# Two probability-value products behind each other in an attention plus SwiGLU kernel

## The chip, the cores and the metric

The kernel runs on one core of a Trainium2 chip. A core has a matrix engine (PE, which loads weights with its own instruction, PEld), a vector engine (DVE), a scalar engine (ACT), a general engine (POOL) and a queue engine (SP) that here only issues DMAs. PE writes to PSUM, eight banks of 512 fp32 columns over 128 partitions; DVE and ACT move results from there to SBUF. Each engine runs its own instructions in the order of the program, and semaphores keep them in step. The metric is the device time of one execution in microseconds: 559.44 us, median of three runs (559.44 to 559.45).

## What is computed

The reference, cut to what matters (S = 2048 tokens, D = 576, H = 32 heads of 18, window W = 256, F = 4608):

```python
xn = layernorm(x)
q, k, v = split(xn @ wqkv)                  # 32 heads of 18
p = softmax(where(0 <= i - j < 256, q @ k.T * 18 ** -0.5, -1e9))
a = (p @ v) @ wo
h = silu(xn @ w1) * (xn @ w3)
out = x + a + h @ w2
```

## The kernel before, in words

The tokens are taken in four chunks of 512 (c = 0 to 3). A chunk has three stretches on PE. First come the projections of q, k and v (chunk 0's stand ahead of the loop). Then come 36 *units* (u = 0 to 35), one for each 128 of the 4608 hidden features. Then a second phase, here called p2, multiplies the hidden features hT by w2 and the attention's output oT by wo, both into the same four PSUM banks, and writes the chunk out.

**A unit** is nine pairs of matmuls, n = 0 to 8 (`unit_pairs`, L697). Each pair uses the two halves of the array at once, 64 rows each, with 512 columns of tokens; one half of the pair makes the gate, the other the up product, in two PSUM banks. Then ACT makes a tanh of the gate (`unit_tanh`, L706), and two DVE instructions make gs and then hT (`unit_h`, L712 and L715). The attention is dealt out between these pairs, so that ACT, DVE and POOL have time for it.

**Attention.** The 32 heads form eight groups g of four. For a group and a chunk there are five steps (four in chunk 0). A step is a few score matmuls into PSUM banks 6 and 7 (`scores`, L571), one exp on ACT (`exps`, L580, from both banks into one *slot* of 1024 bf16 per partition) and one or two masks on POOL (L607). When both groups of a pair j are through, a *PV* (`pv`, L628) multiplies the probabilities with the values. It uses another split of the array: eight tiles of 64 rows and 20 columns, 96 matmuls in chunks 1 to 3, 72 in chunk 0, into two banks. A chunk has four PVs, j = 0 to 3. The last one stands at the start of p2, behind four small matmuls (`wo_rest`, L683).

**Behind a PV** DVE transposes both banks out (`pv_out`, L637, into the buffers `uqs`, the second of which lies in the output tiles `ofin`); then for each half a reciprocal on DVE (L642) and a product on POOL (`o_scale`, L643) and transposes back in two halves per group (`o_turn`, L650, called turns here) into `od`. DMAs pack `od` into oT (`o_pack`, `o_rest`). `later(u, ...)` puts these off, so that they stand behind `unit_h` of unit u, u + 1, u + 2 and u + 3.

**PSUM banks.** Six banks form three pairs that `job()` hands out in turn: to units, PVs and projections. So a unit or a PV takes the banks of the third last one, and PE waits until DVE has read these.

**The order** is written by a planner. `clock` counts time on PE in pair times: 1 for a pair or a step of scores, 6.6 for a PV. `spaced_step` (L955) spreads the steps of scores evenly over what is left of the chunk, at least 7.5 apart, as long as a slot is free; one may also be put ahead of a unit's last pair. A PV is put behind the first unit that ends 20 after the last step that it needs:

```python
if next_pv in pv_ready and clock >= pv_ready[next_pv] and next_pv < 3:
    ...
    later(u, lambda b=banks: (pv_out(b[0], 0), pv_out(b[1], 1), o_scale(0)))
```

In chunks 1 and 2 the planner puts the PVs 0, 1 and 2 behind units 8, 16 and 24, in chunk 3 behind 8, 17 and 26.

**Slots.** The first four steps of a chunk use the hT tiles of units 28 to 35, which are written only then. After that come ten slots of `pt` and, in chunks 1 to 3, four in `stage`; a PV gives its `pt` and `stage` slots back.

**DMAs.** SP issues nearly all of them in order, each after the semaphores that it needs. w1 and w3 come in parts (`load_part`), w2 in 72 tiles of 512 x 288, 288 KB each, through four buffers: whenever p2 is through with a tile, `load_w2` (L338, called in `p2_item`) loads the one four further on, at the end of p2 the first four of the next chunk. Chunk 0's first four load at units 20 to 26.

**The next chunk's tokens** are normalised during the units: statistics at units 20, 24, 30 and 34 (`ln_stats`, L353 to L356), applied at 22, 26, 32 and 35 (`ln_apply`, L378) on DVE, and turned by a DMA (`xn_send`) at 23, 27, 33 and in p2. Chunk 3 has none of this.

## Time and profile before

| what | value |
|---|---|
| median of three runs | 559.44 us |
| span of the profiled execution | 557.72 us |
| PE busy | 553.1 us, 99% |
| DVE, ACT, POOL busy | 309.6, 259.4, 163.3 us |
| chain that ended last | PE 98%, DMA 1% |
| granted PE clock | 9 tenths or more in all 40 slices |
| DMA, mean | 154 GB/s |
| w2 tile, issue to landing | 3.4 us median |

The profile is of one execution. Its span, 557.72 us, is 1.72 us less than the runs' median; the rest lies ahead of its first and behind its last instruction. The page reports matmuls as busy from their start to a modelled end, so overlapping matmuls make PE look busy throughout. Lost time on PE is therefore read from the starts: a matmul of N columns keeps its part of the array for N columns, and what lies beyond that until the next start is lost. The line with the chain says what the end of the kernel hung on. In lines of the timeline the first number is the start in us, the second the length, and a bracket at the end says how long the engine was idle before it and what released it.

### The profile page before, as it was taken

The page shows a single profiled execution, that of the slowest core. Times are in us where ns is not written, and L with a number is a line of the kernel's source. Part 1 is how long each engine was busy: PE and PEld are TensorE (multiplying, and loading weights), DVE is VectorE, ACT ScalarE, POOL GpSimd, SP SyncE. Part 2 cuts the span into 40 slices and gives each one's busy share as a digit, 9 for nine tenths or more (in the row PEclk, how much of TensorE's full clock was granted, in tenths as well). Part 3 has the DMA queues.
Part 4 walks back from the last instruction along what each step waited for, and adds up shares of the span by engine and source line. Part 5 has one row for each costly group of instructions (what it writes and reads, how often), then busy time and mean ns, then how long its engine had stood idle before and what let it go on. Part 6 is the DMA issues. An engine that isn't in the chain of part 4 may idle for free.

```text
span 557.7 us, 15727 instructions
## 1 busy us (share of the span) xinstructions
PE 553.1 (99%) x6766; PEld 332.9 (60%) x6766; DVE 309.6 (56%) x578; ACT 259.4 (47%) x357; POOL 163.3 (29%) x389
## 2 busy tenths in 40 slices
PE   8999999999999999999999999999999999999998
PEld 4445545787655455477764554548776555455776
DVE  6465889610365778851056668884105577777211
ACT  6457776100387776500048777650005776765000
POOL 5513454300034445330003444423001343432000
PEclk9999999999999999999999999999999999999999
DMA  9987989978576358466956744966593673562552
GB/s 234 228 177 179 207 141 196 165 201 225 135 139 146 110 139 188 125 144 174 238 107 139 166 115 113 182 153 140 151 249 78 135 172 98 129 142 54 139 149 65
DMA packets 127072, 85.96 MB, mean 154 GB/s; under 512 B 34179, under 2 KB 124763, under 8 KB 127003
## 3 DMA queue, kind: packets, MB, share of 16 engines
q1 hardware_dynamic: 125011, 82.69, 64.5%
q10 hardware_dynamic: 1992, 2.27, 1.7%
q8 instruction: 53, 0.87, 0.7%
q14 instruction: 16, 0.13, 0.1%
HBM read 71.29 MB, written 2.36 MB: 132 GB/s over the span
## 4 chain that ended last, share of the span: by engine, by line
PE 98%; DMA 1%; DVE 0%; ACT 0%; issue 0%; POOL 0%
PE ps L697 50%; PE ps L757 25%; PE ps L445 9%; PE ps L571 6%; PE ps L628 4%; PE ps L763 3%; DMA xp<-in_A_x_dram 1%; PE ps L683 0%; PE ps L390 0%; DVE xn L370 0%; ACT stage L825 0%; ACT xnT L397 0%; DVE stats L353 0%; DVE ofin L770 0%; POOL xn L373 0%
## 5 line engine op out<-in xcount | busy, mean ns | idle before, releaser
L697 PE MATMUL ps<-xnT,w 64*128 64x512 bf16 x1400 | 182.9, 376 | 0.0
L697 PE MATMUL ps<-xnS,w 64*128 64x512 bf16 x1120 | 150.9, 376 | 0.0
L757 PE MATMUL ps<-w,hT 128*128 128x288 bf16 x1152 | 146.6, 286 | 0.0
L712 DVE SCALAR_TENSOR_TENSOR gs<-th,ps 128x512 bf16<-128x512 bf16 x144 | 98.0, 681 | 81.4 <-ACT th L706 80.8
L580 ACT ACTIVATE pt<-ps 128x1024 bf16<-128x1024 f32 (+1 forms) x112 | 113.2, 1010 | 53.5 <-PE ps L571 53.0
L757 PEld LDWEIGHTS ps<-w,hT 128*128 128x128 bf16 x1152 | 112.3, 98 | 29.0 <-issue 0.2
L607 POOL TENSOR_TENSOR pt<-pt,mk 128x128 int32<-128x128 int32 (+1 forms) x199 | 80.8, 428 | 79.2 <-ACT pt L580 79.2
L697 PEld LDWEIGHTS ps<-xnT,w 64*128 64x128 bf16 x1400 | 66.5, 94 | 62.8 <-issue 0.3
L706 ACT ACTIVATE th<-ps 128x512 bf16<-128x512 f32 x144 | 85.5, 594 | 35.3 <-PE ps L697 34.7
L715 DVE SCALAR_TENSOR_TENSOR hT<-gs,ps 128x512 bf16<-128x512 bf16 x144 | 98.9, 687 | 4.9
L697 PEld LDWEIGHTS ps<-xnS,w 64*128 64x128 bf16 x1120 | 53.8, 94 | 54.3
L770 DVE TENSOR_TENSOR ofin<-ps,xp 128x288 bf16<-128x288 f32 x32 | 13.8, 455 | 124.9 <-PE ps L763 66.8
L458 ACT ACTIVATE stage<-ps 128x512 bf16<-128x512 f32 x16 | 9.5, 596 | 142.0 <-PE ps L445 139.7
L607 POOL TENSOR_TENSOR hT<-hT,mk 128x128 int32<-128x128 int32 (+1 forms) x31 | 12.4, 422 | 164.3 <-ACT hT L580 164.3
L571 PE MATMUL ps<-qv,kv 64*128 64x320 bf16 (+4 forms) x528 | 51.5, 260 | 0.0
L571 PEld LDWEIGHTS ps<-qv,kv 64*128 64x128 bf16 x528 | 25.3, 94 | 28.1 <-ACT hT L580 1.7
L445 PE MATMUL ps<-xnT,wp 64*128 64x512 bf16 (+1 forms) x360 | 37.9, 355 | 0.0
L650 DVE STREAM_TRANSPOSE od<-oq 128x256 bf16<-128x256 bf16 x64 | 25.8, 427 | 7.0 <-POOL oq L643 7.0
L580 ACT ACTIVATE stage<-ps 128x1024 bf16<-128x1024 f32 x24 | 24.6, 1024 | 10.2 <-PE ps L571 10.0
L445 PEld LDWEIGHTS ps<-xnT,wp 64*128 64x128 bf16 x360 | 18.9, 94 | 14.5
L643 POOL TENSOR_TENSOR oq<-uq,rden 128x288 bf16<-128x288 f32 x16 | 10.8, 673 | 40.7 <-DVE rden L642 40.7
L445 PE MATMUL ps<-wv,xnT 64*128 64x288 bf16 x288 | 22.2, 283 | 0.1
(75 smaller groups left out, 345.4 us busy)
## 6 DMA issues: line engine op xcount, KB each, us to landing
w<-in_B_w_dram SPq DMA_DIRECT2D x208, 192.0 KB, 4.2
w<-in_B_w_dram SPq DMA_DIRECT2D x72, 288.0 KB, 3.4
xp<-in_A_x_dram SPq DMA_DIRECT2D x30, 144.0 KB, 3.5
out_dram<-ofin SPq DMA_DIRECT2D x32, 72.0 KB, 2.0
xnS<-xnT SPq DMA_DIRECT2D x8, 256.0 KB, 6.6
oT<-od SPq DMA_DIRECT2D x40, 36.0 KB
pt<-in_A_wqkv_dram SPq DMA_DIRECT2D x4, 288.0 KB, 6.8
hT<-in_B_w_dram SPq DMA_DIRECT2D x6, 192.0 KB, 4.2
```

The lines of the kernel that those rows point to most:

```text
L445: op = add("pe", lambda e, out_=out_, st=st, mv=mv, n=n, r0=r0, first=first: e.matmul(out_, st, mv, start=first, stop=(part == 1 and n == ...
L571: add("pe", lambda e, r0=r0, out_=out_, kb=kb, q0=q0, nb=nb: e.matmul(out_, kb4[r0:r0 + 64, g, kb + NV - NB, :] if kb < 0 else kv[r0:r0 + ...
L580: add("act", lambda e: e.activation(pt_slot(sl)[:, 0:w, :], PS[:, SC[0]:SC[1] + 1, 0:w].rearrange("p r q -> p q r"), ACT.Exp, scale=scale) ...
L607: add("pool", lambda e, vb=vb, mm=mm: e.tensor_tensor(vb, vb, mm, ALU.mult), r=(key if n == 0 else []) + ["mk"], **{"w" if n == 0 else "j" ...
L628: add("pe", lambda e, p=p, q=q, pr=pr, sl=sl, g=g, pos=pos, q0=q0, nb=nb, col=col, first=first, n=n: e.matmul(PS[32 * q:32 * q + VW, banks ...
L650: add("dve", lambda e: e.transpose(od[i][:, g % 2, c0:c0 + CH // 2], oq[:, c0:c0 + CH // 2]), r=["oq", "oq0"], **{"j" if half or g % 2 els ...
L697: op = add("pe", lambda e, n=n, r0=r0, r=r, k=k, src=src: e.matmul(PS[:, b0 + r, :], wt[r0:r0 + 64, k, fl * 128:(fl + 1) * 128], src, star ...
L706: add("act", lambda e: e.activation(th[i][:], PS[:, bg, :], ACT.Tanh, scale=0.5), r=[("ps", bg)], w=[("th", i)])
L712: add("dve", lambda e: e.scalar_tensor_tensor(out=gs[i][:], in0=th[i][:], scalar=1.0, in1=PS[:, bg, :], op0=ALU.add, op1=ALU.mult), r=[("t ...
L715: add("dve", lambda e: e.scalar_tensor_tensor(out=hT[:, u, :], in0=gs[i][:], scalar=0.5, in1=PS[:, bu, :], op0=ALU.mult, op1=ALU.mult), r= ...
L757: add("pe", lambda e: e.matmul(bank, hT[:, f, tt * 128:(tt + 1) * 128], w2[sl][:, k, :], start=(f == 0 and half == 1), stop=False), r=[("h ...
L763: add("pe", lambda e: e.matmul(bank, oT[:, k, tt * 128:(tt + 1) * 128], wo[:, k, d0:d0 + HD], start=False, stop=(k == 3 and (half == 0 or ...
```

## The change

In chunks 1, 2 and 3 two PVs stand directly behind each other at a place that a table gives: (first PV, unit, pair ahead of which they stand).

- `JOINT`: chunk 1, PVs 1 and 2 in unit 27 ahead of pair 7; chunk 2, PVs 0 and 1 in unit 18 ahead of pair 4; chunk 3, PVs 1 and 2 in unit 27 ahead of pair 8. The remaining PV of the three goes where the planner puts it; the last PV and chunk 0 are as before.
- All four `pv_out` and the first `o_scale` stand right behind the two PVs, ahead of the unit's own `unit_h`. The turns, packs and other scales are put off to units u to u + 5. The second PV's transposes go into two slots that the first PV gave back (`kept`); they come free at u + 3.
- The job counter goes one further, so that the next unit gets the first PV's banks.
- Slots: steps 4 to 9 of chunks 1 and 3 use the four w2 buffers and both `od` buffers, in chunk 2 two w2 buffers and both `od`. In chunks 1 and 3 two `stage` slots are held for steps 30 and 31, and the hT and w2 slots of PV 0 are used a second time.
- p2 no longer loads the first four w2 tiles of the next chunk (for chunk 2: it loads the first two). They load at units 27, 29, 31 and 33 of chunks 1 and 3, and at units 20 and 24 of chunk 2.

```diff
@@ pt_slot, pt_keys
+            if kind == "w2":
+                return w2[n][:, :, :].rearrange("p f d -> p (f d)")[:, 0:2 * CH].rearrange("p (q r) -> p q r", r=2)
+            if kind == "od":
+                return od[n][:, :, :].rearrange("p g c -> p (g c)").rearrange("p (q r) -> p q r", r=2)
...
@@ load_w2
-        def load_w2():
+        def load_w2(upto):
             nonlocal n2fill
-            if n2fill >= NC * 2 * NFC:
+            if n2fill >= min(upto, NC * 2 * NFC):
                 return
@@ p2_item
-                    load_w2()
+                    load_w2((c + 1) * 2 * NFC + (2 if c + 1 < NC and JOINT[c + 1][0] == 0 else 0))
@@ the loop over chunks
+        JOINT = {1: (1, 27, 7), 2: (0, 18, 4), 3: (1, 27, 8)}
...
             if c:
-                free += [("sh", n) for n in range(4)]
+                free += [("sh", n) for n in range(4 if JOINT[c][0] == 0 else 2)]
             early = [("h", n) for n in range(4)]
+            if c:
+                early += [("w2", (c * 2 * NFC + n) % NW2) for n in range(2 if JOINT[c][0] == 0 else 0, 4)] + [("od", n) for n in range(NOD)]
+            held = {} if c == 0 or JOINT[c][0] == 0 else {6 * NS: ("sh", 2), 6 * NS + 1: ("sh", 3)}
...
+            def release(j, kept):
+                for g in (2 * j, 2 * j + 1):
+                    for st in range(NS):
+                        sl = pt_of[(c, g, st)]
+                        ok = ("pt", "sh", "h", "w2") if c and at_u < 22 and JOINT[c][0] == 1 else ("pt", "sh")
+                        if sl[0] in ok:
+                            (kept if kept is not None and len(kept) < 2 and sl[0] in ("pt", "sh") else free).append(sl)
...
+                    if c and (u, n) == JOINT[c][1:]:
+                        ja = JOINT[c][0]
+                        assert next_pv == ja and ja + 1 in pv_ready and clock >= pv_ready[ja + 1], (c, next_pv, clock, pv_ready)
+                        two = [job(), job()]
+                        job_ctr += 1
+                        kept = []
...
+                        for m, j in enumerate((ja, ja + 1)):
+                            pv(c, j, two[m])
+                            clock += PV_COST
+                            release(j, kept)
+                        next_pv = ja + 2
+                        for m, sl in enumerate(kept):
+                            uqs[2 + m:] = [pt_slot(sl).rearrange("p q r -> p (q r)").bitcast(dt.float32)]
+                            uq_keys[2 + m:] = [pt_keys(sl)]
+                        pv_out(two[0][0], 0)
+                        pv_out(two[0][1], 1)
+                        o_scale(0)
+                        pv_out(two[1][0], 2)
+                        pv_out(two[1][1], 3)
+                        g = 2 * ja
+                        later(u, lambda g=g: (o_turn(g, 0), o_turn(g, 1), o_scale(1)))
+                        later(u + 1, lambda g=g: o_turn(g + 1, 0))
+                        later(u + 2, lambda g=g, ja=ja: (o_turn(g + 1, 1), o_pack(ja, "sp"), o_scale(2)))
+                        later(u + 3, lambda g=g: (o_turn(g + 2, 0), o_turn(g + 2, 1), o_scale(3)))
+                        later(u + 3, lambda kept=kept: free.extend(kept))
+                        later(u + 4, lambda g=g: o_turn(g + 3, 0))
+                        later(u + 5, lambda g=g, ja=ja: (o_turn(g + 3, 1), o_pack(ja + 1, "sp")))
...
-                if next_pv in pv_ready and clock >= pv_ready[next_pv] and next_pv < 3:
+                if (c == 0 or next_pv not in (JOINT[c][0], JOINT[c][0] + 1)) and next_pv in pv_ready and clock >= pv_ready[next_pv] and next_pv < 3:
...
-                if c == 0 and u in (20, 22, 24, 26):
-                    load_w2()
+                if u in ((20, 22, 24, 26) if c == 0 else (JOINT[c][1] + 2, JOINT[c][1] + 6) if JOINT[c][0] == 0 else (27, 29, 31, 33)):
+                    load_w2(c * 2 * NFC + 4)
```

More of the change, by code (lines that the diff above doesn't have):

```diff
@@ L244, in pt_keys @@
             kind, n = sl
-            if kind == "pt":
-                return [("pt", n)]
+            if kind in ("pt", "w2", "od"):
+                return [(kind, n)]
             if kind == "sh":
@@ L636, in pv_out @@
         def pv_out(b, i):
-            add("dve", lambda e: e.transpose(uqs[i], PS[:, b, :]), r=[("ps", b)], w=uq_keys[i])
+            add("dve", lambda e, to=uqs[i]: e.transpose(to, PS[:, b, :]), r=[("ps", b)], w=uq_keys[i])
         def o_scale(i):
@@ L941, in take @@
                     return early[n]
+                if n in held:
+                    return held[n]
                 return free.pop(0)
@@ L990, in bass_parallel_sum__sliding_block__glu_gated_swiglu__prompt_kernel @@
                     into = nxt - (clock + 9 - n)
-                    if done < len(att) and (free or done < len(early)) and (clock >= nxt or (n == 8 and into < 3 and clock >= soon)):
+                    if c and (u, n) == JOINT[c][1:]:
[4 more added lines that the diff above has]
+                        kept = []
+                        _DEBUG.setdefault("joint", []).append((c, u, n, done, round(clock - pv_ready[ja + 1], 1), len([o for o in P.ops if o.eng == "pe"])))
+                        for m, j in enumerate((ja, ja + 1)):
[19 more added lines that the diff above has]
+                        later(u + 5, lambda g=g, ja=ja: (o_turn(g + 3, 1), o_pack(ja + 1, "sp")))
+                        if ja == 0:
+                            for m in range(7):
+                                later(u + 4 + m // 2 + m // 6, lambda m=m: o_rest(m, "sp"))
+                    if done < len(att) and (free or done < len(early) or done in held) and (clock >= nxt or (n == 8 and into < 3 and clock >= soon)):
                         spaced_step()
@@ L1005, in bass_parallel_sum__sliding_block__glu_gated_swiglu__prompt_kernel @@
                     clock += PV_COST
-                    for g in (2 * j, 2 * j + 1):
-                        for s in range(NS):
-                            if pt_of[(c, g, s)][0] != "h":
-                                free.append(pt_of[(c, g, s)])
+                    release(j, None)
                     later(u, lambda b=banks: (pv_out(b[0], 0), pv_out(b[1], 1), o_scale(0)))
```

## The prediction

> **What bounds the kernel.** I read the page's first and fourth part, then single instructions of PE around the PVs, then DVE at the ends of the unit phases. (A PV multiplies one head group pair's probabilities with the values; a unit is one block of 128 hidden features; "h" is a unit's last DVE instruction, on hT.)

> ```profile
> PE 553.1 (99%) x6766; PEld 332.9 (60%) x6766; DVE 309.6 (56%) x578; ACT 259.4 (47%) x357; POOL 163.3 (29%) x389
> PE 98%; DMA 1%; DVE 0%; ACT 0%; issue 0%; POOL 0%
> ```

> PE is the path, with 98% of the chain that ended last. So the change can only gain where PE itself loses time, and every wait it puts on PE costs in full. Where does PE lose time now? The timeline of PE around the first PV of chunk 1, the last unit pair ahead of it and the scores behind it (start, us, instruction):

> ```profile
> 175.75 0.38 PE L697 MATMUL ps<-xnT,w 64*128 64x512 bf16 x2
> 176.05 0.31 PE L628 MATMUL ps<-hT,va 64*20 64x320 bf16 x2
> ...
> 177.16 0.27 PE L628 MATMUL ps<-pt,va 64*20 64x256 bf16 x1
> 177.36 0.31 PE L571 MATMUL ps<-qv,kv 64*128 64x320 bf16 x2
> ```

> Unit pairs of 512 columns start 0.216 us apart (nine pairs from 236.61 to 238.56 in the trace), so the pair at 175.75 has streamed by 175.96, and the PV, another split of the array (64x20 for 64x128), starts 0.09 later. Its last matmul starts at 177.16 and streams 256 columns, 0.11, to 177.26; the scores start 0.09 to 0.10 later. I worked this out so for all matmuls. Past the start of the kernel, about the only losses over 0.06 us are these: 0.092 to 0.094 going into each of the 12 PVs between units, 0.094 to 0.103 coming out. No wait for DVE, ACT or a DMA shows there. Of the 557.7 us, the change can touch these 0.19 us per PV, no more.

> The last view is DVE at the end of chunk 1's units. Unit 30 is at 230.16, the statistics of the next chunk's tokens at 231.49, unit 34 at 237.45:

> ```profile
> 230.16 0.69 DVE L712 SCALAR_TENSOR_TENSOR gs<-th,ps 128x512 bf16<-128x512 bf16 x1 [0.75 <-ACT th L706]
> 230.88 0.69 DVE L715 SCALAR_TENSOR_TENSOR hT<-gs,ps 128x512 bf16<-128x512 bf16 x1
> 231.49 0.45 DVE L353 BATCH_NORM_STATS2 stats<-xp 128x6 f32<-128x288 bf16 x1
> ...
> 236.31 0.69 DVE L715 SCALAR_TENSOR_TENSOR hT<-gs,ps 128x512 bf16<-128x512 bf16 x1
> 237.45 0.69 DVE L712 SCALAR_TENSOR_TENSOR gs<-th,ps 128x512 bf16<-128x512 bf16 x1 [0.45 <-ACT th L706]
> 238.17 0.69 DVE L715 SCALAR_TENSOR_TENSOR hT<-gs,ps 128x512 bf16<-128x512 bf16 x1
> ```

> ```profile
> 238.68 0.29 PE L683 MATMUL ps<-wo,oT 64*128 64x288 bf16 x2
> 238.91 0.32 PE L628 MATMUL ps<-stage,va 64*20 64x320 bf16 x4
> ```

> The chunk's last PV (238.91) reuses unit 34's PSUM banks. Unit 34's h ends at 238.86, 0.05 before it: already nothing is to spare, and what makes that h later makes PE later.

> **The change, part by part.** The sum is against the profiled execution, span 557.72; the median, 559.44, is 1.72 more, which lies outside the span and is left as it is.

> *Two PVs behind each other, three times.* One exit and one entry of the array split go: 0.095 + 0.093 = 0.19 per place, 3 x 0.19 = 0.57 off PE. The matmuls are the same ones. What a second PV costs behind another one no row shows. Of the twelve PVs of chunks 1 to 3, eleven stream for 1.20 to 1.22 from first start to last end, and one, at 471.76, for 1.31. Its eight array tiles stream 2560 columns each, 1.07 at the rate above, so a second PV might save up to 0.09 of the ragged start and end, or lose the 0.10 of the slow one. The ordinary row is nearest: 0, with plus and minus 0.3 for the three as range.

> *The second PV's banks, chunk 2 (unit 18, ahead of pair 4).* It takes unit 17's banks. From a unit's last pair to the end of its h: unit 34 streams until 236.61, h ends at 238.86, 2.24. In unit 18 there come four pairs (0.86), the entry (0.09) and one PV (some 1.15 to where the next could start): 2.10 to 2.12. PE waits about 0.15 (with 0.05 from DVE's end to PE's start, as above). In chunks 1 and 3 seven and eight pairs come first, 0.65 and more over: nothing.

> *The next unit's banks.* An extra step of the job counter gives unit u+1 the first PV's banks, whose two transposes (216.18 to 216.81, 0.63 each to the next start) end some 1.5 after that PV, 0.2 of it PE to DVE. Unit u+1 starts after the second PV, the exit, a score and the rest of the unit: 1.74 (chunk 3), 1.95 (1), 2.6 (2). This holds with 0.2 to spare at the least.

> *Evacuation moved late, chunk 1.* Two PVs leave at unit 27 what had been left at units 16 and 24. After unit 30 DVE gets these in addition: two turns and a reciprocal (220.68 to 221.51, 0.83), and one turn behind each of units 31 and 32 (222.84 to 223.20, 0.36): 1.55. Unit 30's gs waits for ACT in both kernels: by the planner's counter a score falls ahead of its last pair, as in the rows, and by then DVE is 1.3 free. Cover: from 231.49 DVE is busy without a gap up to 236.91 (0.60 after the start at 236.31), 0.54 before unit 34's gs could start; and scores that wait for the joint place put three instead of one behind unit 30, two pair times, 0.43 of PE. 1.55 - 0.54 - 0.43 = 0.58: unit 34's h, and with it the last PV, 0.58 later. Ends: 0.2 (if turns run in gaps that I don't see) and 0.9 (an apply took 0.78 instead of 0.55 where POOL ran beside it, 223.20 to 223.98). [...]

> In chunk 3 there are no statistics or applies, and the same working leaves 0.9 to spare. In chunk 2 the joint place lies at 18 and the third PV one unit later than before, at 25; its turns are over by unit 28. Nothing.

> *Scores and probabilities.* Holding two PVs' probabilities takes more slots; that is what W2, od and hT tiles are for, same exp (1.02) and masks. Slots run out for 19 (chunk 1), 8 (2) and 6 (3) pair times ahead of the joint place; then scores come 8 pair times apart, 1.73, in which ACT has 1.02 + 0.60. Chunk 0 has runs at 8 already and no loss at its scores. The last scores come at unit 33 rather than 32 in chunk 1; exp and masks (0.46 each) need 2.5, the PV is 5.6 away. Nothing.

> *W2's first tiles* (four in chunks 1 and 3, two in chunk 2) load from unit 27, or 20, on, where they were loaded during the phase before. On SP they stand behind the packs, which wait for DVE's turns, and in chunk 1 the last one behind a transfer that waits for the apply at unit 32. A tile of 288 KB lands in 3.4 (median), the last is issued some 9 before its use, the others 12 to 16. DMA queues are busy 60% in 223 to 240 us; 1.15 MB more over 17 us are 68 GB/s beside 131. Nothing on PE; without that cover, a late tile would cost PE its lateness. The space freed in the phase before gains nothing, as PE waits for no DMA there.

> Sum: -0.57 + 0.15 + 0.58 = +0.16, 557.88 span, **559.6**.

> **Rivals.**
> *DVE is in time*, at both places. For it: 0.58 is a difference of small terms. 559.44 - 0.57 = 558.9.
> *The array drains between two PVs too.* Then only half or none of the 0.19 is won. Against it: within a PV, matmuls on all eight tiles follow without such a gap. 559.6 + 3 x 0.10 = 559.9.
> *Slower: evacuation holds PE at every joint place*, as in chunk 1. 559.6 + 2 x 0.58 = 560.8. It decides as soon as DVE is later than the next need by over 0.9 in chunk 3 and some 0.5 in chunk 2. Against it: DVE is busy 13.28 of 17.2 at chunk 3's end, 14.90 of 17.30 at chunk 1's. [...]
> *Slower: PE outruns its instructions.* A joint place has 384 in 2.4 us. The trace's instruction queue fetches 16 KB at a time, about one per 256 of PE's instructions (53 fetches), each 0.9 to 1.7 us. If it had fewer than some 200 ahead, PE would stand for one fetch at each place, about 1.2: 559.6 + 3.6 = 563.2. Against it: sixteen PVs of 144 or 192 instructions, fifteen without a hitch. [...]

> **How the numbers follow.** Main case 0.49, DVE in time 0.28, drains 0.09, evacuation 0.06, instructions 0.05; 0.03 for what no row shows. 0.2% is 1.1 us here, about what can be told from no change. No case reaches 558.3 (all three places at their best: 559.44 - 0.57 - 0.27 = 558.6), so faster has 0.02 of the rest; slower 0.06 + 0.05 + 0.01 = 0.12; same 0.86. The range runs from 558.8 to 560.4: the main case with its ends (0.58 as 0.2 or 0.9, the second PVs 0.3 either way), DVE in time, and drains; 0.13 is left out.

> **What would show it.** Three places with no gap between 192 PV matmuls, and 13 exits of PVs instead of 16. In chunk 1 the last PV starts some 0.6 after the pair of L683 matmuls more than in chunk 3, with a wait for DVE's hT; in unit 18 of chunk 2 a gap of about 0.15 between the PVs. No PE wait for a DMA. I am wrong if PE loses time elsewhere: at a score (slots or ACT), at the first w2 matmul (a tile late), or inside a second PV.

## The result, and the profile after

The changed kernel takes 563.66 us (median of six runs, 561.61 to 564.32) where the kernel before, in runs beside it, takes 559.61. The ratio is 1.0063, interval 1.0047 to 1.0079: slower by 0.6%. The profiled execution took 563.35 us with a span of 561.63, which is 3.91 more than before.

The page of the changed kernel, busy time and the chain that ended last:

```profile
PE 554.8 (99%) x6766; PEld 333.1 (59%) x6766; DVE 309.3 (55%) x578; ACT 259.4 (46%) x357; POOL 163.1 (29%) x389
PE 96%; DVE 2%; issue 1%; ACT 0%; DMA 0%; SPq 0%; POOL 0%; DVEq 0%
```

The instructions are the same in number, but the chain now runs for 2% of the span over DVE. To find the place I cut the span at the first projection matmul of chunks 1, 2 and 3. These lengths, each from the one execution that a run's profile holds, are the measure in all that follows. They repeat well: chunk 2 took 137.49 to 137.58 in the five executions in which its instructions are those of the kernel before. The PE instructions of chunk 0 don't change, but the next chunk began 142.2 to 144.3 us into the profiled executions (those without added matmuls), mostly through waits for the first loads; that alone moves the whole time by as much as the change was meant to win.

| us | chunk 1 | chunk 2 | chunk 3 |
|---|---|---|---|
| before | 137.50 | 137.51 | 140.44 |
| after | 137.80 | 141.53 | 140.07 |
| difference | +0.30 | +4.02 | -0.37 |

**The joint itself.** The timeline of PE of the changed kernel around the two PVs of chunk 1 (start, length, instruction):

```profile
217.34 0.81 PE L701 MATMUL ps<-xnS,w 64*128 64x512 bf16 x6
218.08 1.37 PE L632 MATMUL ps<-pt,va 64*20 64x320 bf16 x96
219.24 0.32 PE L632 MATMUL ps<-stage,va 64*20 64x320 bf16 x4
...
220.31 0.34 PE L632 MATMUL ps<-w,va 64*20 64x256 bf16 x4
220.58 0.31 PE L575 MATMUL ps<-qv,kv 64*128 64x320 bf16 x2
```

The second PV starts 1.16 after the first, and both stream for 2.40 in all (2.38 in chunk 3); in the profile before, a single PV takes 1.20 to 1.22 and loses 0.19 around it. So the part of the change that was meant to gain gains: 0.19 a place, and some 0.03 more because the second PV fills the ragged end of the first.

**Chunk 1's end.** DVE of the changed kernel, and PE at the last PV. In brackets is the idle time and what ended it:

```profile
235.46 0.44 DVE L654 STREAM_TRANSPOSE od<-oq 128x256 bf16<-128x256 bf16 x1
235.82 0.60 DVE L382 TENSOR_SCALAR xn<-xp,mv,rstd 128x576 bf16<-128x576 bf16 x2
236.33 0.68 DVE L716 SCALAR_TENSOR_TENSOR gs<-th,ps 128x512 bf16<-128x512 bf16 x1
...
237.65 0.68 DVE L716 SCALAR_TENSOR_TENSOR gs<-th,ps 128x512 bf16<-128x512 bf16 x1
238.37 0.69 DVE L719 SCALAR_TENSOR_TENSOR hT<-gs,ps 128x512 bf16<-128x512 bf16 x1
```

```profile
238.32 0.41 PE L687 MATMUL ps<-wo,oT 64*128 64x288 bf16 x4
239.11 0.32 PE L632 MATMUL ps<-stage,va 64*20 64x320 bf16 x4 [0.38 <-DVE hT L719]
```

DVE comes out of turns, statistics and applies without a pause, unit 34's h ends at 239.06, and the last PV loses 0.55 on PE, against 0.11 before: +0.44.

**Chunk 2's loss.** DVE, and below it SP, of the changed kernel around units 26 to 28:

```profile
359.84 0.69 DVE L719 SCALAR_TENSOR_TENSOR hT<-gs,ps 128x512 bf16<-128x512 bf16 x1
363.23 0.77 DVE L654 STREAM_TRANSPOSE od<-oq 128x256 bf16<-128x256 bf16 x2 [2.71 <-DMA oT<-od]
363.92 0.21 DVE L646 RECIPROCAL rden<-ofin 128x16 f32<-128x16 f32 x1
364.06 0.90 DVE L382 TENSOR_SCALAR xn<-xp,mv,rstd 128x576 bf16<-128x576 bf16 x2
364.88 0.67 DVE L716 SCALAR_TENSOR_TENSOR gs<-th,ps 128x512 bf16<-128x512 bf16 x1
365.59 0.69 DVE L719 SCALAR_TENSOR_TENSOR hT<-gs,ps 128x512 bf16<-128x512 bf16 x1
```

```profile
345.87 1.63 SPq L658 DMA_DIRECT2D oT<-od  x2
347.54 0.47 SPq L349 DMA_DIRECT2D w<-in_B_w_dram  x1
348.06 2.68 SPq L322 DMA_DIRECT2D w<-in_B_w_dram  x4
350.79 6.67 SPq L658 DMA_DIRECT2D oT<-od  x8
357.50 1.29 SPq L407 DMA_TRANSPOSE xnT<-xn  x1
358.83 1.35 SPq L322 DMA_DIRECT2D w<-in_B_w_dram  x2
360.23 1.37 SPq L658 DMA_DIRECT2D oT<-od  x2
```

The third PV's first turn writes `od[0]`. It stands still for 2.71 us, because two small transfers that still read `od[0]` for PV 0 land only at 363.15. They are two of the seven that `o_rest` makes, called rests from here on. The diff as shown ahead leaves out the lines that place them:

```diff
+                        if ja == 0:
+                            for m in range(7):
+                                later(u + 4 + m // 2 + m // 6, lambda m=m: o_rest(m, "sp"))
```

For m = 4 and 5 that is unit 24, which is over by 352. SP issued them at 360.23 and 360.98. It had been held at PV 0's pack until DVE's turn (345.87, a wait of 3.1 by SP's own waits), and from there it issued in program order with one pause of 0.5: 20 DMAs up to 361.60, 0.8 each on average. In the profile before, the first and the third PV of chunk 2, which share `od[0]`, start 38 us apart (313.55 and 351.62), now 20 (334.12 and 353.88). There the same two rests went out at 332.91, and the third PV's first turn 25 us later waits for nothing (SP, then DVE, of the kernel before):

```profile
332.91 1.38 SPq L654 DMA_DIRECT2D oT<-od  x2
```

```profile
358.17 0.76 DVE L650 STREAM_TRANSPOSE od<-oq 128x256 bf16<-128x256 bf16 x2
```

What follows on PE, timeline and then a cut by windows (busy time and count of PE, PEld, DVE, ACT, POOL, then the granted clock, the DMA share and GB/s):

```profile
363.85 0.38 PE L701 MATMUL ps<-xnT,w 64*128 64x512 bf16 x2
366.33 1.08 PE L701 MATMUL ps<-xnT,w 64*128 64x512 bf16 x8 [2.10 <-DVE hT L719]
...
368.07 1.47 PE L701 MATMUL ps<-xnS,w 64*128 64x512 bf16 x6
```

```profile
364.00:366.30 2.30, 0.23 (x4) 0.00 (x0) 2.27 (x6) 1.24 (x2) 2.09 (x5) 1.00 0.95 262
366.30:371.50 5.20, 5.17 (x42) 2.29 (x44) 4.03 (x8) 1.65 (x3) 1.29 (x4) 0.67 1.00 172
```

Behind the turn stand a reciprocal, two applies and unit 27's gs and hT. Unit 30 of PE needs unit 27's banks, so PE stands from 364.06 (the pair at 363.85 has then streamed) to 366.33, 2.27 us. Then the granted clock is 0.67 over 5.20 us, which costs 0.33 x 5.20 = 1.7 more; the clock's records in the trace show 0.5 for 3.41 us from 367.20. Six 512-column matmuls take 1.47 there, and 0.81 elsewhere. Not every execution has this: in four of the six the mean clock was 0.996 to 0.999, in two, 561.61 and 563.50 us, it was 1.0.

So chunk 2: -0.19 (joint), +0.21 (the second PV waits for unit 17's banks, as predicted 0.15), +2.27, +1.7 = +4.0, measured +4.02. Chunk 1: -0.19 - 0.03 + 0.44 = +0.22, measured +0.30; two ragged PVs (1.24 and 1.26 us for 1.21) are the rest. Chunk 3: -0.22, and 0.10 because the PV of 1.31 in the profile before is an ordinary one here: -0.32, measured -0.37.

### The profile page after: what moved, and what is told of

The parts are those of the page before. It is cut to its first block, busy times and chain, and to the rows that moved or that the text cites. A ratio compares the mean times of both kernels' runs of the same rounds, so it can differ in the third digit from the quotient of the medians.

```text
span 561.6 us, 15732 instructions
## 1 busy us (share of the span) xinstructions
PE 554.8 (99%) x6766; PEld 333.1 (59%) x6766; DVE 309.3 (55%) x578; ACT 259.4 (46%) x357; POOL 163.1 (29%) x389
## 3 DMA queue, kind: packets, MB, share of 16 engines
q10 hardware_dynamic: 1992, 2.27, 1.7%
## 4 chain that ended last, share of the span: by engine, by line
PE 96%; DVE 2%; issue 1%; ACT 0%; DMA 0%; SPq 0%; POOL 0%; DVEq 0%
PE ps L701 48%; PE ps L761 25%; PE ps L449 9%; PE ps L575 6%; PE ps L632 3%; PE ps L767 3%; PE ps L796 1%; DVE gs L716 1%; DVE hT L719 1%; DVE od L654 0%; DMA oT<-od 0%; PE ps L687 0%; DVE xn L382 0%; PE ps L394 0%; ACT stage L829 0%
## 5 line engine op out<-in xcount | busy, mean ns | idle before, releaser
L701 PE MATMUL ps<-xnS,w 64*128 64x512 bf16 x1120 | 153.4, 378 | 0.0
L584 ACT ACTIVATE pt<-ps 128x1024 bf16<-128x1024 f32 (+1 forms) x88 | 88.6, 1006 | 47.0 <-PE ps L575 46.6
L611 POOL TENSOR_TENSOR pt<-pt,mk 128x128 int32<-128x128 int32 (+1 forms) x156 | 63.1, 429 | 43.7 <-ACT pt L584 43.7
L611 POOL TENSOR_TENSOR hT<-hT,mk 128x128 int32<-128x128 int32 (+1 forms) x45 | 18.3, 427 | 173.9 <-ACT hT L584 173.9
L584 ACT ACTIVATE hT<-ps 128x1024 bf16<-128x1024 f32 (+1 forms) x24 | 24.4, 1015 | 6.2 <-PE ps L575 5.9
L584 ACT ACTIVATE w<-ps 128x1024 bf16<-128x1024 f32 x18 | 18.4, 1023 | 6.1 <-PE ps L575 5.9
```

The source lines that it names most:

```text
L584: add("act", lambda e: e.activation(pt_slot(sl)[:, 0:w, :], PS[:, SC[0]:SC[1] + 1, 0:w].rearrange("p r q -> p q r"), ACT.Exp, scale=scale) ...
L611: add("pool", lambda e, vb=vb, mm=mm: e.tensor_tensor(vb, vb, mm, ALU.mult), r=(key if n == 0 else []) + ["mk"], **{"w" if n == 0 else "j" ...
L701: op = add("pe", lambda e, n=n, r0=r0, r=r, k=k, src=src: e.matmul(PS[:, b0 + r, :], wt[r0:r0 + 64, k, fl * 128:(fl + 1) * 128], src, star ...
```

## The experiments

The theory at the outset, A: chunk 2's loss is the turn that waits for `od[0]`, because SP is late. Its rivals: C, SP's queue as such, so that something else that SP issues comes late once `od` is out of the way; H, the w2 tiles that load in the units, by their bandwidth or their place in the queue; F, PE's supply of instructions, which the prediction had named.

### One joint at a time

The table of places was cut down; a chunk that isn't in it runs its four PVs by the planner, as before, with its own slots and w2 loads.

```diff
-        JOINT = {1: (1, 27, 7), 2: (0, 18, 4), 3: (1, 27, 8)}
+        JOINT = {1: (1, 27, 7), 3: (1, 27, 8)}      # first run
+        JOINT = {2: (0, 18, 4)}                     # second
+        JOINT = {3: (1, 27, 8)}                     # third
```

> The changed kernel with chunk 2 as in the kernel before (no joint place, its w2 tiles loaded in the phase before); chunks 1 and 3 keep theirs. Theory A (all that is lost comes from chunk 2's joint place: the third PV's turn waits there for DMAs that still read the same od buffer, DVE stands 2.7 us, PE 2.3 and then runs at half clock for 3.4): 559.44 - 2 x 0.19 + 0.44 (chunk 1's last PV, late by its h) = 559.5. Rival B (each joint place holds engines or SP's queue up, and chunk 2 is only where it shows): 561 or more, with waits in chunks 1 or 3.

> Chunk 2's joint place alone, chunks 1 and 3 as in the kernel before. Theory A: 559.44 - 0.19 + 0.21 (the second PV waits for its banks) + 2.27 (PE's stand in unit 30) + 1.6 (half clock) = 563.3. Rival B: about a third of the change's loss, 560.8.

> Chunk 3's joint place alone, the undisturbed one in the profile. One exit and one entry of the array split saved, the second PV at its ordinary price: 559.44 - 0.19 = 559.25. If the array drained between two PVs, or the second cost more: 559.35 to 559.45.

| | chunk 1 | chunk 2 | chunk 3 | median | ratio to before |
|---|---|---|---|---|---|
| joints in 1 and 3 | 137.76 | 137.51 | 140.07 | 560.28 | 1.0000 [0.9991, 1.0010] |
| joint in 2 | 137.54 | 140.16 | 140.37 | 563.68 | 1.0061 [1.0046, 1.0077] |
| joint in 3 | 137.51 | 137.49 | 140.08 | 559.58 | 0.9991 [0.9981, 1.0000] |

The loss goes with chunk 2's joint and comes with it. Chunk 3 with its joint is 0.36 shorter; some 0.1 of that is the slow PV of the profile before, which is ordinary in the run with chunk 2's joint alone too (140.37). Chunk 1 with its joint loses 0.26. In the execution profiled with chunk 2's joint alone the wait is as long, but the clock stayed at 1.0: the turn and then PE, two lines of two timelines,

```profile
363.75 0.77 DVE L654 STREAM_TRANSPOSE od<-oq 128x256 bf16<-128x256 bf16 x2 [3.00 <-DMA oT<-od]
```

```profile
366.85 1.04 PE L701 MATMUL ps<-xnT,w 64*128 64x512 bf16 x8 [2.40 <-DVE hT L719]
```

so chunk 2 costs 2.65 rather than 4.02. In the other three executions of that run the mean clock was 0.997, so the ratio in the table has the half clock in it. The half clock is an addition that comes in some executions, not the cause.

### Other buffers for the turns

```diff
+        od_of = [0, 1, 0, 1]
...
-            i = g // 2 % NOD
+            i = od_of[g // 2]
...
+            od_of[:] = [0, 1, 1, 0] if c == 2 else [0, 1, 0, 1]
```

In chunk 2 the third PV now turns into `od[1]`, the fourth into `od[0]`.

> The changed kernel; in chunk 2 the third PV turns into od buffer 1, which two packs read early, and the fourth into buffer 0. The same transfers and waits else. Theory A: no stand of DVE at the turn, no half clock: 559.44 - 0.57 + 0.21 + 0.44 = 559.5. Rival C (SP's queue is full, or the w2 loads in the units take the bandwidth, and whichever work needs a DMA there waits): DVE or PE still waits some 2 us for a DMA in units 26 to 30, 562 or more.

Chunk 2 took 138.62, the ratio was 1.0035 [1.0022, 1.0049]. DVE's wait is gone, but PE of this kernel has a new one:

```profile
371.49 0.82 PE L703 MATMUL ps<-xnT,w 64*128 64x512 bf16 x6 [0.86 <-issue]
```

The row names no releaser, but the trace has it: from 368.89 to 371.43 PE's sequencer waits for a semaphore that parts of w1 and w3 count up, one that is waited on only at the first use of the same buffer, every 12 units. SP issued the last parts from 364.20 to 367.10, in the same row, and the last of them lands at 371.40. So A was right that `od` made the wait, and C that SP's lateness finds another victim: 1.03 of PE in place of 2.27 and the slow clock behind it.

### The late transfers off SP's crowded stretch

Two edits: the rests put off to units 28 to 32 on SP (with the swapped buffers), and, with the buffers as in the change, the rests issued by ACT.

```diff
-                                later(u + 4 + m // 2 + m // 6, lambda m=m: o_rest(m, "sp"))
+                                later(28 + m // 2 + m // 6, lambda m=m: o_rest(m, "sp"))   # first, and od_of
+                                later(u + 4 + m // 2 + m // 6, lambda m=m: o_rest(m, "act")) # second
```

> The run with the other od buffer, and besides chunk 2's seven small transfers of the rest (o_rest) are put off from units 22 to 25 to units 28 to 32, so that six of them no longer stand ahead of w1 and w3 parts on SP. Theory D (SP's own issue rate is what runs out behind chunk 2's joint place: some 29 DMAs at 0.6 to 0.8 us each between units 20 and 28): the wait of 1.03 us at unit 32 for a part of w1 or w3 goes; chunk 2 takes 138.62 - 1.03 = 137.6. Rival E (the DMA queues are too slow for the parts with the w2 tiles added): chunk 2 stays at 138.4 or more.

> The changed kernel, od buffers as they are; chunk 2's seven transfers of the rest are issued by ACT instead of SP. Theory D: they go out as soon as the turns are made, so DVE's wait of 2.7 us at the third PV's turn and PE's stand go; ACT has 0.55 us more for each, which may show as a PE wait of up to 1 us. Chunk 2 at 137.6 to 138.6 instead of 141.53. If the od reuse itself were too close, whoever issues: a DVE wait of over 1 us at that turn stays.

The first missed: chunk 2 took 140.13, and the ratio was 1.0087 [1.0063, 1.0112], with a mean clock of 0.996 to 0.997 in three of its four executions, though not in the one profiled. The wait for w1 and w3 is gone, as it should be if SP's row of issues made it (D) and not slow transfers (E), but the last rest now comes too late for the output's matmuls. The second took 138.33, 1.0019 [1.0010, 1.0029]: DVE no longer waits for a DMA at all, with the very buffers of the change, so what mattered was when the transfers were issued. ACT, though, is put back by issuing (1.26 for the first two), and a score waits. PE in the one and the other:

```profile
379.41 0.41 PE L689 MATMUL ps<-wo,oT 64*128 64x288 bf16 x3 [2.28 <-DMA oT<-oT]
```

```profile
349.96 0.28 PE L575 MATMUL ps<-qv,kb 64*128 64x256 bf16 x2 [0.48 <-ACT pt L584]
```

### The w2 loads later

```diff
-                if u in ((20, 22, 24, 26) if c == 0 else (JOINT[c][1] + 2, JOINT[c][1] + 6) if JOINT[c][0] == 0 else (27, 29, 31, 33)):
+                if u in ((20, 22, 24, 26) if c == 0 else (30, 32) if JOINT[c][0] == 0 else (27, 29, 31, 33)):
```

> The changed kernel with chunk 2's two w2 tiles loaded at units 30 and 32 instead of 20 and 24. Theory D: they are two of the some 29 DMAs that SP issues there, one of them ahead of the transfers that the turn waits for: DVE's wait of 2.7 becomes some 2.2, chunk 2 at 139.5 or more (with half clock 141). Rival H (the w2 tiles' 576 KB in the units are the cause, by bandwidth): the wait goes, chunk 2 at 138 or less.

DVE waits 2.87 at the turn, PE stands 2.43 at the same place, the clock falls to 0.5 for 3.41 us, and chunk 2 takes 141.62 (563.76 us, one run): H falls. D's 2.2 for DVE was missed too: with one w2 tile fewer ahead of them, the two rests still went out at 360.55.

### Chunk 1's joint two units and one unit earlier

The next runs were to free chunk 1's last PV by an earlier place, so that turns and statistics don't meet. The first of them also has swapped buffers and rests at units 28 and later, and chunk 2's place one pair later.

```diff
+        JOINT = {1: (1, 25, 7), 2: (0, 18, 5), 3: (1, 27, 8)}   # first run
+        JOINT = {1: (1, 25, 7), 2: (0, 18, 4), 3: (1, 27, 8)}   # second
+        JOINT = {1: (1, 26, 7), 2: (0, 18, 4), 3: (1, 27, 8)}   # third
```

> Other od buffer and late rests in chunk 2, chunk 2's joint place one pair later (ahead of pair 5), chunk 1's two units earlier (unit 25, ahead of pair 7). Expected: no PE wait but the array splits; each joint place saves 0.19 and 0.03 of the second PV's start: chunks 1 to 3 at 137.28, 137.29 and 140.07, together 0.8 less than before; ratio 0.9985.

> The changed kernel with chunk 1's joint place in unit 25 instead of 27, chunk 2 and 3 as they are. The last PV's wait for unit 34's h in chunk 1 (0.44 us beyond the array split) comes from turns that stand behind unit 30: with them over by unit 30 it goes, and chunk 1 takes 137.80 - 0.44 = 137.36 or less. If it came from the scores' later places, it stays.

> The changed kernel with chunk 1's joint place in unit 26 ahead of pair 7. Theory F (PE has two blocks of 256 instructions at hand; the next is usable some 3.7 us after a block is begun): in the counts of the two runs with unit 25 the block borders lie 16 and 272 instructions into the joint place and PE stood 2.0 in the second PV; in unit 27 they lie at -56 and 200 and it did not. At unit 26 they lie at -20 and 236, which PE would reach 20/18.5 + 236/160 = 2.55 us apart: it stands 1.1 us in the second PV. Rival G (the stand in unit 25 came from a slot or a mask not ready): nothing in unit 26 or a wait at another place.

| joint of chunk 1 | chunk 1 | chunk 2 | time |
|---|---|---|---|
| unit 25, with the other edits | 141.47 | 139.90 | 566.43, ratio 1.0119 [1.0104, 1.0134] |
| unit 25 | 140.80 | 139.99 | 566.74, one run |
| unit 26 | 137.61 | 140.47 | 562.47, one run |

The last PV's wait is gone in all three: it loses 0.11, as in the profile before. But both runs with unit 25 are worse, and in the same odd way (the ratio of the first includes a mean clock of 0.997 in three of its four executions). PE stands in the middle of the second PV, where no matmul waits for a semaphore, and again in p2, where w2 tiles come late (behind packs on SP that wait for DVE). PE of the second run:

```profile
219.73 0.23 PE L632 MATMUL ps<-hT,va 64*20 64x128 bf16 x4 [1.66 <-issue]
...
248.70 2.13 PE L761 MATMUL ps<-w,hT 128*128 128x288 bf16 x16 [0.90 <-DMA w<-in_B_w_dram]
```

In both the stand begins at the same instruction of PE, matmuls, weight loads and waits for semaphores counted together: number 5313. PE's instruction queue fetches 16 KB at a time, one fetch per 256 or so (53 fetches for 13,627 instructions in the changed kernel). If a block ends at 5313, the one before ended 16 instructions into the joint's 384 (two PVs of 96 matmuls and 96 weight loads): two borders lie inside the joint. At the places of the change the borders lie 56 ahead and 200 into it, and at unit 26, 20 ahead and 236 into it; there PE nowhere stands for its instructions. The number I had expected of F at unit 26 was thus wrong; that place has a wait of 0.28 for unit 25's banks instead, behind DVE's statistics. Chunk 2's later place in the first run works, the wait for unit 17's banks is gone, but the rests at units 28 and later cost 2.44 there, as before.

### Are the stands PE's blocks of 256?

Small matmuls of 64 columns, whose result nothing uses, were added at the start of the kernel. They move the borders and leave all that follows in its order:

```diff
+        for k in range(30):        # 60 instructions with the weight loads; 90 in the second run
+            add("pe", lambda e: e.matmul(PS[:, 4, 0:64], oq[:, 0:128], oq[:, 0:64], start=True, stop=True), r=["oq0"], j=[("ps", 4)])
```

The first run has chunk 1's joint at unit 25, the second joints in chunks 1 and 3 at the recorded places.

> Chunk 1's joint at unit 25, where PE stood 1.83 us inside the second PV, with 60 small PE instructions added at the start of the kernel, which move the borders of PE's blocks of 256 instructions from 16 and 272 into the joint to 44 ahead of it and 212 into it. If the stand is PE's instruction supply: it goes, and no stand over 0.6 us is left inside the joint. If it is a buffer or DVE's mask there: the stand stays, 1.5 to 2.0 us in the second PV.

> Joints in chunks 1 and 3 at the places of the change, where PE stood nowhere for its instructions, with 180 small PE instructions added at the start, which move the borders of the blocks of 256 from 56 ahead and 200 into chunk 1's joint to 20 and 276 into it, and to about 31 and 287 in chunk 3. If two borders inside the joint make the stand: 1.5 to 2.0 us inside the second PV in both chunks, chunk 1 at 139.3 to 139.8 and chunk 3 at 141.6 to 142.1. If instruction supply has nothing to do with it: 137.8 and 140.07 as without the added instructions.

The two runs took 567.35 and 566.54 us (one execution each). With 60 more, the stand of 1.83 at unit 25 is gone: the two PVs take 2.40 again, and chunk 1 takes 138.27, with 0.75 of waits for w2 tiles left in p2. With 180 more, PE stands inside the joints that had run clean. Chunk 1 and chunk 3 of the second run:

```profile
224.58 0.23 PE L632 MATMUL ps<-hT,va 64*20 64x128 bf16 x2 [1.51 <-issue]
```

```profile
502.37 0.20 PE L632 MATMUL ps<-hT,va 64*20 64x64 bf16 x4 [0.77 <-issue]
```

That is 1.67 and 0.93 of PE (expected 1.5 to 2.0 in both), chunk 1 at 139.43, chunk 3 at 141.06. The moved borders made three more stands where there had been none: 1.56 and 0.71 just behind the joints of chunks 2 and 3 in the first run, and 1.34 in a single PV of chunk 2 in the second. All five lie within two instructions of a border by the count fixed at 5313. In chunk 1 of the second run the border before is at 221.14, the fetch goes from 222.22 to 223.36, and PE runs on at 224.58; over all the stands but one, a block came into use 2.6 to 3.8 us after PE had crossed the border ahead of it, and a joint uses 256 instructions in 1.6 us. The one is the single PV: its fetch began 3.2 us after the border, so the place is not all; why it began late I can't say.

### Chunk 1's statistics earlier, and all three together

```diff
             near = {0: (20, 22, 23), 1: (24, 26, 27), 2: (30, 32, 33), 3: (34, 35, 40)}
+            if c == 1:
+                near[2] = (23, 25, 26)   # first and second run
+                near = {0: (10, 12, 13), 1: (14, 16, 17), 2: (18, 20, 21), 3: (34, 35, 40)}   # third and fourth
```

(`near` gives for each 128 tokens of the next chunk the units of statistics, apply and sending.) The first and third run have joints in chunks 1 and 3 alone. The second and fourth have all three, chunk 2's one pair later at (0, 18, 5), with the swapped buffers, and the rests on ACT:

```diff
+                                later((27, 28, 29, 30, 34, 34, 33)[m], lambda m=m: o_rest(m, "act"))   # second
+                                later((27, 28, 29, 30, 33, 34, 32)[m], lambda m=m: o_rest(m, "act"))   # fourth
```

> Joint places in chunks 1 and 3 alone, and in chunk 1 the third tile's statistics and apply at units 23 and 25 instead of 30 and 32 (its transfer at 26), where DVE has no PV to evacuate. Theory A: the 1.5 us that they took behind unit 30 were what made unit 34's h late; the wait of 0.44 at chunk 1's last PV goes. Chunk 1 at 137.50 - 0.23 = 137.3, chunk 3 at 140.07, together 0.6 less than before: ratio 0.999. If the turns alone made it late, some 0.2 to 0.4 of the wait stays.

> As the run before it, and chunk 2's joint place too: one pair later (ahead of pair 5), the other od buffer for its third PV, and the seven small transfers of the rest issued by ACT, one each at units 27 to 30, three at 33 and 34. If SP's issue rate was what chunk 2 lacked: no wait in chunk 2 but the array splits and some 0.1 for ACT, chunk 2 at 137.3; together 0.8 less than before, ratio 0.9985. If not, chunk 2 is over 137.6.

> Joints in chunks 1 and 3 alone, chunk 2 as in the kernel before, and chunk 1's statistics all at earlier units, after PVs that end sooner. If the waits of chunk 1 (0.44 us at the last PV, 0.50 us at the second PV where only the third tile's plan was moved) are all DVE's statistics: both go, chunk 1 takes 137.27 us, chunk 2 137.51, chunk 3 140.07, and the kernel is 0.6 us shorter than before, a ratio of 0.999. If they are the turns' or the masks' time on DVE: chunk 1 stays at 137.6 to 137.85 and the ratio at 1.000.

> All three joints: chunk 1's statistics early, chunk 2's second place one pair later, its third and fourth turn in swapped buffers, and its o_rest transfers issued by ACT, the last of them one unit sooner than in the run before. If SP's late queue is all that made chunk 2's joint dear: no wait over 0.2 us is left in chunk 2, it takes 137.3 us, chunks 1 and 3 137.27 and 140.07, ratio 0.9986. If ACT's own work is put back by the issues: a wait of 0.4 to 0.7 us at a score or at the first output matmul, chunk 2 at 138.0 to 138.3, ratio 1.000 to 1.001.

| | chunk 1 | chunk 2 | chunk 3 | ratio to before |
|---|---|---|---|---|
| 1 and 3, one tile's statistics early | 137.85 | 137.51 | 140.08 | 0.9999 [0.9990, 1.0008] |
| all three, same | 137.87 | 138.16 | 140.10 | 1.0012 [1.0004, 1.0021] |
| 1 and 3, three tiles early | 137.44 | 137.58 | 140.10 | 0.9995 [0.9986, 1.0004] |
| all three, three tiles early | 137.38 | 137.36 | 140.09 | 0.9998 [0.9990, 1.0007] |

With one tile's statistics earlier the last PV's wait is gone, as expected, but chunk 1 took 137.85 for the 137.3 expected, because the crowd has only moved: unit 26's h is late and the second PV waits 0.50. The second run also missed its 137.3 for chunk 2, as the last rest came late for the output's first matmul (0.43). With three tiles moved to units 10 to 20 both waits are gone, and no row of the waits of PE is left past chunk 0. DVE of the third run, where it had been full:

```profile
235.69 0.69 DVE L716 SCALAR_TENSOR_TENSOR gs<-th,ps 128x512 bf16<-128x512 bf16 x1 [0.28 <-ACT th L710]
...
237.63 0.69 DVE L716 SCALAR_TENSOR_TENSOR gs<-th,ps 128x512 bf16<-128x512 bf16 x1 [0.53 <-ACT th L710]
```

Unit 34's gs now waits for ACT, not behind other DVE work. The fourth run has all three joints and no wait: with the rest that the output needs one unit sooner, the wait at that matmul went too. Its chunks 1 to 3 sum to 414.83, the kernel before to 415.45: 0.62 less, some 0.1 of it the slow PV of the profile before, and near the 0.57 that the prediction gave the joints. In the whole time that is a ratio of 0.9998, no change that can be told; 0.62 is 0.11%. Chunk 1 is 0.1 to 0.2 longer than I expected in the third and fourth, 0.06 to 0.13 of it in the last PV (1.27 and 1.34 us for 1.21).

## Why the prediction was wrong

It said 559.6, 558.8 to 560.4, and no change with 0.86. Step by step:

- **Exits and entries: right.** 0.19 a place, three times; the second PV gains about 0.03 where it said 0.
- **Chunk 2's second PV: right.** 0.21 for 0.15. One pair later it is gone, as it must be if it was for unit 17's banks.
- **Chunk 1's evacuation: right mechanism, a little too much.** 0.44 for 0.58. Turns and statistics make it together: it went when only the third tile's statistics were moved, it went when only the joint stood one or two units earlier, and chunk 3, which has no statistics, never had it (with its joint alone PE waits for nothing past chunk 0). So evacuation was the limit at this place; for every joint place, as in the prediction's rival, that fails at chunk 3.
- **Next unit's banks, scores and slots, W2's first tiles: nothing, right.** No wait at a score, at a w2 matmul or at the next unit's banks in the changed kernel; loading chunk 2's w2 tiles later brought nothing (PE stood 2.43 for 2.27).
- **Chunk 2's turns: "its turns are over by unit 28. Nothing." This is the step that failed.** It asked when DVE would be through, not when it could begin. The turn of the third PV has to wait until PV 0's transfers have read `od[0]`, and the joint brings the two PVs from 38 to 20 us apart. For W2's tiles the prediction did say that SP's queue stands behind packs that wait for turns, but it followed only the tiles along that queue and not the rests. The price: 2.27 of PE, and 1.7 more where the clock fell, for a term of nothing. Nor was it among the signs of being wrong that the prediction listed (a score, the first w2 matmul, inside a second PV): PE waited for a unit's banks. That SP's hold at the pack and the 20 DMAs behind it both count is read from the trace; no run took away the one without the other.
- **The rival for slower, evacuation at every place,** had the right chain from there on (late DVE, then PE at unit 30) but would have been 0.58 a place, not 4 at one.
- **The rival on instructions** did not occur in the changed kernel, and was put at 1.2 a place; that its 563.2 lies near the measured 563.66 is chance. It is real elsewhere: PE stood 0.7 to 2.0 us where a border fell badly. I had given it 0.05, and the fifteen PVs without a hitch were no ground for so little: in the second padded run a single PV stood 1.34. No run shows that PE holds more than the block in use and the next, and the stands fit these two (in chunk 1 of that run a border at 221.14, the fetch from 222.22 to 223.36, PE past the next border at 224.58).

What stays open: why one fetch began 3.2 us after its border, and what makes the last PV of chunk 1 ragged in the last two runs. What brings the half clock in one execution and not in another is read from the traces below; no run tested it.

## What to carry to other kernels

When two consumers of a buffer are moved closer together, follow each reader of that buffer to the queue that issues it, and ask when that queue gets there: a DMA queue held for 3 us by one wait was 8 us behind the plan 20 DMAs on. On a path where one engine is 98% busy, moving work needs the slack of every other engine at the new place; a gain of 0.6 us was there, but only with statistics, transfers and buffers moved as well. Measure such a gain in stretches between fixed instructions, as the whole time hides it.

## What the runs showed of the hardware

**PE's instructions came in blocks of some 256** (53 fetches of 16 KB for 13,627 instructions in the changed kernel), and where PE stood for one, it was ready mostly 2.6 to 3.8 us after the border before it (up to 5.9 once). The joints, dense stretches of small matmuls that use 256 instructions in 1.6 us, outran that in some runs, and whether they did hung on how many instructions stood ahead of them in the whole kernel: 60 matmul and weight-load instructions at the start took one stand of 1.83 us away, 180 brought stands of 1.67 and 0.93.
